# Attention backward for one decode query: two bf16 row tiles transposed as one fp32 block, and five dk stores that spare two DMA engines in place of eight

## The chip, the cores and the metric

The kernel runs on one core of a Trainium2 chip. The metric is device time in microseconds (us) of one execution; the time before is the median of three runs, 1280.13 us (1279.72 to 1282.18). The engines are named as the profile names them: PE is TensorE's matrix multiplication, PEld its weight loads, DVE is VectorE, ACT is ScalarE, POOL is GpSimd and SP is SyncE. Here SP issues the loads and POOL the stores.

## The reference

It is softmax attention with one query per head, and its backward pass. There are 2 x 32 = 64 independent heads; each has 8192 keys and values of 128 elements, all bf16.

```python
def _fwd_reference(q, k, v):          # q: 2,32,1,128   k, v: 2,32,8192,128
    scale = q.shape[-1] ** -0.5
    scores = jnp.einsum("bhqd,bhkd->bhqk", q, k) * scale
    p = _softmax(scores, axis=-1)
    return jnp.einsum("bhqk,bhkd->bhqd", p, v)

def reference(q, k, v, grad_out):
    _out, _vjp = jax.vjp(_f, q, k, v)
    return (out, *_vjp(grad_out))     # out, dq, dk, dv
```

For one head, with s = K q and dp = V g (g is the row of grad_out): p = softmax(scale s), out = p V, ds = p (dp - sum(p dp)), dq = scale ds K, dk = scale ds q^T, dv = p g^T. Each head reads K and V (2 MB each) once and writes dk and dv (2 MB each) once, so at least 537 MB move.

## The kernel before

**Tiles.** K or V of one head is one tile `kvt`, 128 partitions x 64 row tiles (NT) x 128 elements: partition p holds 64 consecutive rows of the head. There are 12 such buffers (NTILE), so loads can run six heads ahead. The gradient is written over the tile it belongs to (`outer`, L421: an outer product of the head's q or g row with the weights, on DVE, in place), and the store sends that same buffer out; a load into the buffer has to wait until that store has landed.

**Steps.** The main loop (L456) runs over steps of one chunk, 16 row tiles (CH). A head has eight steps, four chunks of K (w = 0) and four of V (w = 1). Four heads are under way at once: in one step PE does the transposes of one head, the score matmuls one step later, and the accumulations `acc` of an older head, while DVE does the outer products of an older one still. Everything in the loop is pinned to program order, so each engine works its instructions off in the order in which the loop writes them.

**One step on PE.** `transpose_chunk` (L189): 16 transposes of a 128 x 128 bf16 block each (L194). The K or V block is the stationary operand (a weight load, PEld L194), the identity the moving one. The result `tp` fills two PSUM buffers in turn; ACT copies it to SBUF as `ev` (L196). After the transposes come, where they are due, `join` (L409), then four `acc` matmuls (L372; 64 columns of the array each, so two run side by side), `spread_rows` (L228), `max_spread` (L251), and at last `score_chunk` of the step before (L208): four matmuls on 32 columns of the array each, side by side, whose moving operand is a contiguous quarter of `ev` and whose stationary operand is a 32-column window of `qdT`, in which only one column is the head's q (or g) and the rest are zeros, so that chunk c's scores fall into row c.

**The chain inside a head.** After the four K chunks `keep_raw` (L221, DVE) copies the scores out of PSUM, `spread_rows` brings them to one per partition and row tile, then come `max_part` (DVE L240), `max_all` (PE L244, an fp32 transpose of a 128 x 1 column; DVE L246), `max_spread` (PE L251, DVE L261), `expo` (ACT L271, which stands in ACT's order behind the step's copy L196; then DVE L280 fills `E_pad`), and the `acc` matmuls of the next step need `E_pad`. PE L178 (`broadcast`) writes the same PSUM tile `sw` that DVE L240 reads.

**Queues.** SP issues loads (L100) in program order, each waiting for the store that frees its buffer. POOL issues the 2 MB stores (L445). The last head's stores go out in 512 KB pieces on SP. A 128-row transfer gives each of the 16 DMA engines eight rows of 16 KB. `by_rows` (L85), used for dk of the heads in SPREAD (4, 11, ..., 53: eight of them), sends 126 rows in one transfer, nine to each of 14 engines, and two rows in a second, one to each of the two engines left out. [...]

Of the kernel before, what the change touches and what calls it, by code (L numbers as in the profile page):

```python
# [9 lines left out]
ALU = mybir.AluOpType  # L10
AX = mybir.AxisListType
BF16 = mybir.dt.bfloat16
F32 = mybir.dt.float32

CH = 16
QT = 4
CW = 64
NG = 2
SG = 4
SW = 32  # L20
NTILE = 12
FIRST = 6
SPREAD = range(4, 60, 7)


@with_exitstack
def kernel(
# [11 lines left out]
    nc = tc.nc  # L39
    B, H, Sq, D = q.shape  # L40
    Sk = k.shape[2]
    P = nc.NUM_PARTITIONS
    assert Sq == 1 and D == P
    BH = B * H
# [3 lines left out]
    NCH = NT // CH  # L48
    SL = 2 * NCH
    scale = float(D) ** -0.5  # L50
# [69 lines left out]
        load(j, 0)  # L120
        load(j, 1)

    ident_bf = const.tile([P, P], BF16)
    masks.make_identity(nc, ident_bf[:])
    ident_f = const.tile([P, P], F32)
    masks.make_identity(nc, ident_f[:])
    ones = const.tile([P, 1], F32)
    nc.vector.memset(ones[:], 1.0)
    groups = [g * P // NG for g in range(NG)]
# [8 lines left out]
    nc.vector.memset(E_pad[:], 0.0)  # L138
    nc.vector.memset(dS_pad[:], 0.0)

    sel4 = const.tile([P, NCH, SG], F32)
    nc.vector.memset(sel4[:], 0.0)
    for g in range(SG):
        nc.vector.tensor_copy(
            out=sel4[g * SW : (g + 1) * SW, :, g],
            in_=ident_f[g * SW : (g + 1) * SW, g * SW : g * SW + NCH],
        )

    Q0 = NCH - 1
    qdT = const.tile([P, 2, Q0 + NCH * BH + SW], BF16)  # L150
    nc.vector.memset(qdT[:], 0.0)
    for w in range(2):
        tps = ps_m.tile([P, BH], BF16, tag=f"acc{w}", name="tps")
        nc.tensor.transpose(tps[:], qd_nat[:BH, w, :], ident_bf[:BH, :BH])
        nc.vector.tensor_copy(
            out=qdT[:, w, Q0 : Q0 + NCH * BH].rearrange("p (i f) -> p i f", f=NCH)[:, :, 0],
            in_=tps[:],
        )

    dqT = const.tile([P, BH], BF16)  # L160
    oT = const.tile([P, BH], BF16)
# [1 line left out]
    def begin(i):  # L163
# [7 lines left out]
        h.lsum = sw[:, 2 * NT + 2 * P : 2 * NT + 2 * P + 2]  # L171
        h.mb = sw[:, 2 * NT + 2 * P + 2 : 2 * NT + 2 * P + 3]

    def broadcast(i, w):

        h = heads[i]
        pin(
            nc.tensor.matmul(  # L178
                h.qbp,
                lhsT=qdT[:, w, Q0 + NCH * i : Q0 + NCH * i + 1].to_broadcast([P, P]),  # L180
                rhs=ident_bf[:],
                start=True,
                stop=True,
            )
        )
        h.qb[w] = small.tile([P, D], BF16, tag=f"qb{w}", name="qb")
        pin(nc.vector.tensor_copy(out=h.qb[w][:], in_=h.qbp))

    def transpose_chunk(i, c):  # L189
        w, c = divmod(c, NCH)  # L190
        src = heads[i].tile[w]
        tp = ps_tp.tile([P, CH, P], BF16, tag="tp", name="tp")
        for t in range(CH):
            pin(nc.tensor.transpose(tp[:, t, :], src[:, c * CH + t, :], ident_bf[:]))  # L194
        ev = evp.tile([P, CH, P], BF16, tag="ev", name="ev")
        pin(nc.scalar.copy(out=ev[:], in_=tp[:]))  # L196
        return ev

    def score_chunk(i, c, ev):

        h = heads[i]
        w, c = divmod(c, NCH)
        if c == 0:
            h.raw = ps_sdp.tile([P, QT * P], F32, tag="raw", name="raw")
        q0 = Q0 + NCH * i - c
        for g in range(SG):
            pin(
                nc.tensor.matmul(  # L208
                    h.raw[g * SW : (g + 1) * SW, :],
                    lhsT=qdT[:, w, q0 : q0 + SW],  # L210
                    rhs=ev[:, g * QT : (g + 1) * QT, :].rearrange("p n d -> p (n d)"),
                    start=(c == 0),
                    stop=(c == NCH - 1),
                )
            )
# [7 lines left out]
    def spread_rows(i, w):  # L223

        h = heads[i]
        for t in range(QT):
            pin(
                nc.tensor.matmul(  # L228
                    h.score[w].rearrange("p (n t) -> p n t", t=QT)[:, :, t],
                    lhsT=h.rows[:, t * P : (t + 1) * P],  # L230
                    rhs=sel4[:].rearrange("p c g -> p (c g)"),
                    start=True,
                    stop=True,
                )
            )

    def max_part(i):
        h = heads[i]
        h.mp = small.tile([P, 1], F32, tag="mp", name="mp")
        pin(nc.vector.reduce_max(out=h.mp[:], in_=h.s, axis=AX.X))  # L240

    def max_all(i):
        h = heads[i]
        pin(nc.tensor.transpose(h.mT, h.mp[:], ident_f[:]))  # L244
        h.gm = small.tile([1, 1], F32, tag="gm", name="gm")
        pin(nc.vector.reduce_max(out=h.gm[:], in_=h.mT, axis=AX.X))  # L246

    def max_spread(i):
        h = heads[i]
        pin(  # L250
            nc.tensor.matmul(  # L251
                h.mb,
                lhsT=ones[0:1, :].to_broadcast([1, P]),
                rhs=h.gm[:],
                start=True,
                stop=True,
            )
        )
        h.negm = small.tile([P, 1], F32, tag="negm", name="negm")
        pin(  # L260
            nc.vector.tensor_scalar(  # L261
                out=h.negm[:], in0=h.mb, scalar1=-scale, scalar2=None, op0=ALU.mult
            )
        )

    def expo(i):
        h = heads[i]
        h.E_f = work.tile([P, NT], F32, tag="E_f", name="E_f")
        h.ld = small.tile([P, 2], F32, tag="ld", name="ld")
        pin(  # L270
            nc.scalar.activation(  # L271
                out=h.E_f[:],
                in_=h.s,
                func=ACT.Exp,
                bias=h.negm[:],
                scale=scale,
                accum_out=h.ld[:, 0:1],
            )
        )
        pin(nc.vector.tensor_copy(out=E_pad[:, 0:NT], in_=h.E_f[:]))  # L280
# [39 lines left out]
    def normalise_p(i):  # L320
        h = heads[i]
        total(h.lsum[:, 0:1], h.ld[:, 0:1])
        h.rl = small.tile([P, 1], F32, tag="rl", name="rl")
        pin(nc.vector.reciprocal(out=h.rl[:], in_=h.lsum[:, 0:1]))
        pairs(i, 1, h.E_f, h.rl[:], "p2")
        h.rls = small.tile([P, 1], F32, tag="rls", name="rls")
        pin(
            nc.vector.tensor_scalar(
                out=h.rls[:], in0=h.rl[:], scalar1=scale, scalar2=None, op0=ALU.mult
            )  # L330
        )

    def normalise_ds(i):
        h = heads[i]
        total(h.lsum[:, 1:2], h.ld[:, 1:2])
        negdelta = small.tile([P, 1], F32, tag="negdelta", name="negdelta")
        pin(
            nc.vector.tensor_scalar(
                out=negdelta[:],
                in0=h.lsum[:, 1:2],  # L340
                scalar1=h.rl[:],
                scalar2=-1.0,
                op0=ALU.mult,
                op1=ALU.mult,
            )
        )
        dSu = work.tile([P, NT], F32, tag="dSu", name="dSu")
        pin(
            nc.vector.scalar_tensor_tensor(
                out=dSu[:],  # L350
                in0=h.dp,
                scalar=negdelta[:],
                in1=h.E_f[:],
                op0=ALU.add,
                op1=ALU.mult,
            )
        )
        pin(nc.vector.tensor_copy(out=dS_pad[:, 0:NT], in_=dSu[:]))  # L358
        pairs(i, 0, dSu, h.rls[:], "ds2")

    def acc(i, w, c):

# [42 lines left out]
    def join(i, w):  # L405

        h = heads[i]
        pin(
            nc.tensor.matmul(h.acc[w][:, 0:1], lhsT=h.sel[:], rhs=ones[:], start=True, stop=True)  # L409
        )  # L410
        pin(
            nc.vector.tensor_scalar(
                out=(oT if w else dqT)[:, i : i + 1],
                in0=h.acc[w][:, 0:1],
                scalar1=(h.rl if w else h.rls)[:],
                scalar2=None,
                op0=ALU.mult,
            )
        )
# [32 lines left out]
    last = list(range(1, NCH + 1))  # L452
    AHEAD = NTILE // 2

    prev = None
    for g in range(SL * BH + O0 + NCH + 4 - SL):  # L456
        now = [(g // SL - b, g % SL + b * SL) for b in range(4)]
# [2 lines left out]
        def at(r0):  # L460

            return next((i for i, r in now if r == r0), None)
# [37 lines left out]
        if prev is not None:  # L500
            score_chunk(*prev)
        prev = (g // SL, g % SL, ev) if ev is not None else None

        if (i := at(NCH)) is not None:
            keep_raw(i)
# [16 lines left out]

    for w, (src, dst) in enumerate(((dqT, out_1), (oT, out_0))):
        tps = ps_m.tile([BH, P], BF16, tag=f"acc{w}", name="tps")
        nc.tensor.transpose(tps[:], src[:], ident_bf[:])
        nat = evp.tile([P, CH, P], BF16, tag="ev", name="nat")
        nc.vector.tensor_copy(out=nat[:BH, 0, :], in_=tps[:])
        load_eng.dma_start(out=dst.rearrange("b h s d -> (b h s) d"), in_=nat[:BH, 0, :])
# [30 lines left out]
```

## Time and profile before

| | before |
|---|---|
| median of three runs (lowest to highest) | 1280.13 us (1279.72 to 1282.18) |
| span of the profiled execution | 1280.2 us |
| mean granted TensorE clock | 0.991 |
| ACT copy ev<-tp L196 | x512, 954.5 us, 1865 ns each |
| DVE outer product L427 | x512, 616.8 us, 1216 ns each |
| PE transposes L194 | x8192, 544.4 us busy, 220 ns each (pipelined) |
| PE scores L208 | x2048, 205.2 us busy |
| PE acc L372 | x2048, 320.0 us busy |
| stores to landing (POOL, 2 MB) | 40.6 us median |
| loads to landing (SP, 2 MB) | 19.1 and 19.4 us median |
| moved | 539.03 MB, mean 421 GB/s |

The span is that of one profiled execution, and it agrees with the median of the runs to 0.1 us. Busy times are unions of records, and a PE record holds the latency of the pipeline too: 16 transposes of 220 ns each take about 0.9 us, not 3.5. How much PE really takes is therefore read from the starts of its groups in the timeline. Idle time of an engine counts only where it holds up the chain that ends last.

### The profile page before, as it was taken

The page shows a single profiled execution, that of the slowest core. Times are in us where ns is not written, and L with a number is a line of the kernel's source. Part 1 is how long each engine was busy: PE and PEld are TensorE (multiplying, and loading weights), DVE is VectorE, ACT ScalarE, POOL GpSimd, SP SyncE. Part 2 cuts the span into 40 slices and gives each one's busy share as a digit, 9 for nine tenths or more (in the row PEclk, how much of TensorE's full clock was granted, in tenths as well). Part 3 has the DMA queues.
Part 4 walks back from the last instruction along what each step waited for, and adds up shares of the span by engine and source line. Part 5 has one row for each costly group of instructions (what it writes and reads, how often), then busy time and mean ns, then how long its engine had stood idle before and what let it go on. Part 6 is the DMA issues. An engine that isn't in the chain of part 4 may idle for free.

```text
span 1280.2 us, 32473 instructions
## 1 busy us (share of the span) xinstructions
PE 1190.2 (93%) x14148; PEld 810.6 (63%) x14148; DVE 1025.8 (80%) x2256; ACT 975.3 (76%) x641; POOL 76.0 (6%) x143
## 2 busy tenths in 40 slices
PE   6999999999999999999999999999999999999994
PEld 5666666666666666666666666666666666666662
DVE  2888887888877888888888878788778888888885
ACT  6777777778777777777777777787777777777771
POOL 0000000000000000000000000000000000000000
PEclk9999999999999999999999999999999999999996
DMA  9999999999999999999999999999999999999996
GB/s 392 423 428 428 428 427 429 430 426 429 427 430 425 414 427 429 428 423 428 428 429 419 425 428 426 427 421 427 427 423 421 427 429 428 420 425 428 428 411 273
DMA packets 40155, 539.03 MB, mean 421 GB/s; under 512 B 5196, under 2 KB 5196, under 8 KB 6476
## 3 DMA queue, kind: packets, MB, share of 16 engines
q1 hardware_dynamic: 20172, 272.70, 50.1%
q0 software_dynamic: 19840, 264.25, 49.0%
q8 instruction: 110, 1.80, 0.5%
q14 instruction: 33, 0.27, 0.1%
HBM read 268.47 MB, written 268.47 MB: 419 GB/s over the span
## 4 chain that ended last, share of the span: by engine, by line
PE 59%; DVE 16%; ACT 10%; issue 10%; DMA 4%; POOL 0%; SPq 0%; ACTq 0%; POOLq 0%; DVEq 0%
PE tp L194 24%; PE acc L372 15%; ACT ev L196 9%; PE raw L208 9%; DVE kvt L427 6%; PE sw L228 4%; DVE sel L395 4%; DMA out_dram<-kvt 3%; DVE rows L221 3%; PE sw L315 3%; PE sw L178 2%; PE acc L409 2%; ACT E_f L271 1%; DVE sel L389 1%; DVE E_pad L280 1%
## 5 line engine op out<-in xcount | busy, mean ns | idle before, releaser
L196 ACT COPY ev<-tp 128x2048 bf16<-128x2048 bf16 x512 | 954.5, 1865 | 275.6 <-PE tp L194 268.9
L427 DVE TENSOR_TENSOR kvt<-qb,pair 128x2048 bf16<-128x2048 bf16 x512 | 616.8, 1216 | 0.2
L194 PE MATMUL tp<-ident_bf,kvt 128*128 128x128 bf16 x8192 | 544.4, 220 | 0.0
L194 PEld LDWEIGHTS <-kvt 128*128 128x128 bf16 x8192 | 482.4, 99 | 81.6 <-issue 80.7
L208 PE MATMUL raw<-ev,qdT 128*32 128x512 bf16 x2048 | 205.2, 391 | 1.5 <-ACT ev L196 1.5
L372 PE MATMUL acc<-kvt,E_pad 128*64 128x512 bf16 x1024 | 160.2, 393 | 24.5 <-DVE E_pad L280 24.5
L372 PE MATMUL acc<-kvt,dS_pad 128*64 128x512 bf16 x1024 | 159.8, 393 | 0.1
L228 PEld LDWEIGHTS sw<-sel,rows 128*128 128x128 f32 x1024 | 124.7, 192 | 52.4 <-DVE sel L395 25.9
L395 DVE SCALAR_TENSOR_TENSOR sel<-acc,diag,sel 128x128 f32<-128x128 f32 x384 | 134.8, 351 | 13.6
L208 PEld LDWEIGHTS <-qdT 128*32 128x32 bf16 x2048 | 53.1, 93 | 136.6 <-issue 131.8
L228 PE MATMUL sw<-sel,rows 128*128 128x16 f32 x1024 | 137.1, 266 | 0.0
L445 POOL DMA_DIRECT2D out_dram<-kvt x118 | 63.3, 536 | 1094.0 <-DVE kvt L427 555.7
L221 DVE COPY rows<-raw 128x512 f32<-128x512 f32 x128 | 88.6, 692 | 22.4 <-PE raw L208 22.4
L280 DVE CAST E_pad<-E_f 128x64 bf16<-128x64 f32 x64 | 12.5, 195 | 80.3 <-ACT E_f L271 80.3
L372 PEld LDWEIGHTS <-E_pad 128*64 128x64 bf16 x1024 | 36.1, 108 | 49.9 <-DVE E_pad L280 35.7
L178 PE MATMUL sw<-ident_bf,qdT 128*128 128x128 bf16 x128 | 28.5, 223 | 38.2 <-DVE mp L240 38.2
L246 DVE TENSOR_REDUCE gm<-sw 1x1 f32<-1x128 f32 x64 | 17.9, 279 | 55.4 <-PE sw L244 55.4
L315 PEld LDWEIGHTS sw<-ld,ones 128*128 128x128 f32 x256 | 38.1, 188 | 29.7 <-issue 15.0
L372 PEld LDWEIGHTS <-dS_pad 128*64 128x64 bf16 x1024 | 36.4, 108 | 22.3 <-DVE dS_pad L358 1.0
L315 PE MATMUL sw<-ld,ones 128*128 128x1 f32 x256 | 49.1, 261 | 0.0
L409 PE MATMUL acc<-ones,sel 128*128 128x1 f32 x256 | 43.3, 239 | 5.3 <-DVE sel L395 5.3
L389 DVE TENSOR_SCALAR sel<-acc,diag 128x128 f32<-128x128 f32 x128 | 43.8, 342 | 0.0
(49 smaller groups left out, 377.1 us busy)
## 6 DMA issues: line engine op xcount, KB each, us to landing
out_dram<-kvt POOLq DMA_DIRECT2D x118, 2048.0 KB, 40.6
kvt<-in_v_dram SPq DMA_DIRECT2D x64, 2048.0 KB, 19.1
kvt<-in_k_dram SPq DMA_DIRECT2D x63, 2048.0 KB, 19.4
out_dram<-kvt POOLq DMA_DIRECT2D x8, 2016.0 KB, 44.9
out_dram<-kvt SPq DMA_DIRECT2D x8, 512.0 KB, 10.9
kvt<-in_k_dram SPq DMA_DIRECT2D x2, 512.0 KB, 4.3
kvt<-in_k_dram SPq DMA_DIRECT2D x1, 1024.0 KB, 6.9
out_dram<-kvt POOLq DMA_DIRECT2D x8, 32.0 KB, 44.3
```

Source lines behind the costliest of these rows:

```text
L194: pin(nc.tensor.transpose(tp[:, t, :], src[:, c * CH + t, :], ident_bf[:]))
L196: pin(nc.scalar.copy(out=ev[:], in_=tp[:]))
L208: nc.tensor.matmul(h.raw[g * SW : (g + 1) * SW, :], lhsT=qdT[:, w, q0 : q0 + SW], rhs=ev[:, g * QT : (g + 1) * QT, :].rearrange("p n d -> ...
L221: pin(nc.vector.tensor_copy(out=h.rows[:], in_=h.raw[:]))
L228: nc.tensor.matmul(h.score[w].rearrange("p (n t) -> p n t", t=QT)[:, :, t], lhsT=h.rows[:, t * P : (t + 1) * P], rhs=sel4[:].rearrange("p ...
L315: nc.tensor.matmul(out, lhsT=ones[:].to_broadcast([P, P]), rhs=col, start=True, stop=True)
L372: nc.tensor.matmul(h.acc[w][g : g + CW, :], lhsT=wts[:, n0 : n0 + CW], rhs=rows[:, n0 : n0 + QT, :].rearrange("p n d -> p (n d)"), start=( ...
L389: nc.vector.tensor_scalar(out=h.sel[:], in0=block, scalar1=diag[:, 0:1], scalar2=None, op0=ALU.mult)
L395: nc.vector.scalar_tensor_tensor(out=h.sel[:], in0=block, scalar=diag[:, b : b + 1], in1=h.sel[:], op0=ALU.mult, op1=ALU.add,)
L409: nc.tensor.matmul(h.acc[w][:, 0:1], lhsT=h.sel[:], rhs=ones[:], start=True, stop=True)
L427: nc.vector.tensor_tensor(out=h.tile[w][:, n0 : n0 + CH, :].rearrange("p n (e t) -> p n e t", t=2), in0=h.qb[w][:] .rearrange("p (e t) -> ...
L445: pin(eng.dma_start(out=dst[:, b0:b1, :], in_=h.tile[w][:, b0:b1, :]))
```

## The change

There are two parts. First, two neighbouring bf16 row tiles (row n and row n + 1 of each partition, 256 elements in a row) are read as 128 fp32 elements, and one fp32 transpose moves both: 8 transposes a chunk in place of 16. Partition j of the result holds, as one fp32 word, elements 2j and 2j + 1 (mod 256) of the pair, so partitions 0 to 63 belong to row n, partitions 64 to 127 to row n + 1, and the low and the high half of the words are even and odd elements. ACT copies 128 x 1024 fp32 words instead of 128 x 2048 bf16 ones. The score matmuls read `ev` as bf16 with a step of two elements, one matmul for each of two halves of the columns and each of even and odd. The stationary operand is a new window `qwin` with two columns of `qpair` (q or g spread over the two halves of the partitions, even and odd), which ACT copies in once per head and w (`window`). `sel4`, `spread_rows` and the set-up are adapted: four more set-up transposes with their copies, and `ident_bf` is now the high half of each word of `ident_f`, so it too is read with a step of two. The seven small per-head tiles become columns of one tile `st`.

Second, SPREAD goes from `range(4, 60, 7)` (eight heads) to `range(6, 60, 12)` (heads 6, 18, 30, 42 and 54).

```diff
-SPREAD = range(4, 60, 7)
+SPREAD = range(6, 60, 12)
...
-    ident_bf = const.tile([P, P], BF16)
-    masks.make_identity(nc, ident_bf[:])
     ident_f = const.tile([P, P], F32)
     masks.make_identity(nc, ident_f[:])
+    ident_bf = ident_f[:].bitcast(BF16).rearrange("p (n e) -> p n e", e=2)[:, :, 1]
...
-    Q0 = NCH - 1
-    qdT = const.tile([P, 2, Q0 + NCH * BH + SW], BF16)
+    Q0 = 2 * NCH - 2
+    qT = const.tile([P, 2, BH], BF16)
+    qpair = const.tile([P, 2, BH, 2, 2], BF16)
+    nc.vector.memset(qpair[:], 0.0)
+    qwin = const.tile([P, 2, 2, Q0 + SW], BF16)
+    nc.vector.memset(qwin[:], 0.0)
+    qd_pair = evp.tile([P, 2, 2, 2, D // 2], BF16, tag="ev", name="qd_pair")
+    for w in range(2):
+        nc.vector.tensor_copy(out=qd_pair[:BH, w], in_=...)
+        for e in range(2):
+            tps = ps_m.tile([P, BH], BF16, tag=f"acc{e}", name="tps")
+            nc.tensor.transpose(tps[:], qd_pair[:BH, w, e]..., ident_bf[:BH, :BH])
+            for t in range(2):
+                half = slice(t * D // 2, (t + 1) * D // 2)
+                nc.vector.tensor_copy(out=qpair[half, w, :, e, t], in_=tps[half, :])
...
+    def window(i, w):
+        pin(nc.scalar.copy(out=qwin[:, w, :, Q0 : Q0 + 2], in_=qpair[:, w, i]))
...
     def transpose_chunk(i, c):
-        tp = ps_tp.tile([P, CH, P], BF16, tag="tp", name="tp")
-        for t in range(CH):
-            pin(nc.tensor.transpose(tp[:, t, :], src[:, c * CH + t, :], ident_bf[:]))
-        ev = evp.tile([P, CH, P], BF16, tag="ev", name="ev")
+        tp = ps_tp.tile([P, CH // 2, P], F32, tag="tp", name="tp")
+        for m in range(CH // 2):
+            n0 = c * CH + 2 * m
+            two = src[:, n0 : n0 + 2, :].rearrange("p n d -> p (n d)").bitcast(F32)
+            pin(nc.tensor.transpose(tp[:, m, :], two, ident_f[:]))
+        ev = evp.tile([P, CH // 2, P], F32, tag="ev", name="ev")
         pin(nc.scalar.copy(out=ev[:], in_=tp[:]))
...
     def score_chunk(i, c, ev):
-        q0 = Q0 + NCH * i - c
+        q0 = Q0 - 2 * c
+        cols = ev[:].rearrange("p m s -> p (m s)").bitcast(BF16)
+               .rearrange("p (b s e) -> p b s e", b=SG // 2, e=2)
         for g in range(SG):
+            b, e = divmod(g, 2)
             pin(
                 nc.tensor.matmul(
                     h.raw[g * SW : (g + 1) * SW, :],
-                    lhsT=qdT[:, w, q0 : q0 + SW],
-                    rhs=ev[:, g * QT : (g + 1) * QT, :].rearrange("p n d -> p (n d)"),
+                    lhsT=qwin[:, w, e, q0 : q0 + SW],
+                    rhs=cols[:, b, :, e],
...
+    window(0, 0)
+    window(0, 1)
     prev = None
     for g in range(SL * BH + O0 + NCH + 4 - SL):
...
         prev = (g // SL, g % SL, ev) if ev is not None else None
+        if (i := at(NCH + 1)) is not None and i + 1 < BH:
+            window(i + 1, 0)
+        if (i := at(1)) is not None and i > 0:
+            window(i, 1)
```

More of the change, by code (lines that the diff above doesn't have):

```diff
@@ L139 @@
     nc.vector.memset(dS_pad[:], 0.0)
-    sel4 = const.tile([P, NCH, SG], F32)
+    sel4 = const.tile([P, NCH, SG // 2, 2], F32)
     nc.vector.memset(sel4[:], 0.0)
@@ L144 @@
         nc.vector.tensor_copy(
-            out=sel4[g * SW : (g + 1) * SW, :, g],
-            in_=ident_f[g * SW : (g + 1) * SW, g * SW : g * SW + NCH],
-        )
-    Q0 = NCH - 1
-    qdT = const.tile([P, 2, Q0 + NCH * BH + SW], BF16)
-    nc.vector.memset(qdT[:], 0.0)
+            out=sel4[g * SW : (g + 1) * SW, :, g // 2, :],
+            in_=ident_f[g * SW : (g + 1) * SW, g * SW : g * SW + 2 * NCH].rearrange(
+                "p (c t) -> p c t", t=2
+            ),
+        )
+    Q0 = 2 * NCH - 2
[6 more added lines that the diff above has]
+    for w in range(2):
+        nc.vector.tensor_copy(
+            out=qd_pair[:BH, w],
+            in_=qd_nat[:BH, w, :]
+            .rearrange("p (j e) -> p e j", e=2)
+            .unsqueeze(2)
+            .to_broadcast([BH, 2, 2, D // 2]),
+        )
+        for e in range(2):
+            tps = ps_m.tile([P, BH], BF16, tag=f"acc{e}", name="tps")
+            nc.tensor.transpose(
+                tps[:],
+                qd_pair[:BH, w, e].rearrange("p t j -> p (t j)"),
+                ident_bf[:BH, :BH],
+            )
+            for t in range(2):
+                half = slice(t * D // 2, (t + 1) * D // 2)
+                nc.vector.tensor_copy(out=qpair[half, w, :, e, t], in_=tps[half, :])
     for w in range(2):
@@ L154 @@
         nc.tensor.transpose(tps[:], qd_nat[:BH, w, :], ident_bf[:BH, :BH])
[L155 to L158, printed above, removed]
+        nc.vector.tensor_copy(out=qT[:, w, :], in_=tps[:])
     dqT = const.tile([P, BH], BF16)
@@ L179, in broadcast @@
                 h.qbp,
-                lhsT=qdT[:, w, Q0 + NCH * i : Q0 + NCH * i + 1].to_broadcast([P, P]),
-                rhs=ident_bf[:],
+                lhsT=qT[:, w, i : i + 1].to_broadcast([P, P]),
+                rhs=ident_bf,
                 start=True,
@@ L204, in score_chunk @@
             h.raw = ps_sdp.tile([P, QT * P], F32, tag="raw", name="raw")
-        q0 = Q0 + NCH * i - c
+        q0 = Q0 - 2 * c
+        cols = (
+            ev[:]
+            .rearrange("p m s -> p (m s)")
+            .bitcast(BF16)
+            .rearrange("p (b s e) -> p b s e", b=SG // 2, e=2)
+        )
         for g in range(SG):
+            b, e = divmod(g, 2)
             pin(
@@ L225, in spread_rows @@
         h = heads[i]
-        for t in range(QT):
+        for m in range(QT):
             pin(
                 nc.tensor.matmul(
-                    h.score[w].rearrange("p (n t) -> p n t", t=QT)[:, :, t],
-                    lhsT=h.rows[:, t * P : (t + 1) * P],
-                    rhs=sel4[:].rearrange("p c g -> p (c g)"),
+                    h.score[w].rearrange("p (n m t) -> p n m t", m=QT, t=2)[:, :, m, :],
+                    lhsT=h.rows[:, m * P : (m + 1) * P],
+                    rhs=sel4[:].rearrange("p c b t -> p (c b t)"),
                     start=True,
@@ L238, in max_part @@
         h = heads[i]
-        h.mp = small.tile([P, 1], F32, tag="mp", name="mp")
-        pin(nc.vector.reduce_max(out=h.mp[:], in_=h.s, axis=AX.X))
+        st = small.tile([P, 8], F32, tag="st", name="st")
+        h.mp, h.gm, h.negm = st[:, 0:1], st[0:1, 1:2], st[:, 2:3]
+        h.ld, h.rl, h.rls, h.negdelta = st[:, 3:5], st[:, 5:6], st[:, 6:7], st[:, 7:8]
+        pin(nc.vector.reduce_max(out=h.mp, in_=h.s, axis=AX.X))
     def max_all(i):
         h = heads[i]
-        pin(nc.tensor.transpose(h.mT, h.mp[:], ident_f[:]))
-        h.gm = small.tile([1, 1], F32, tag="gm", name="gm")
-        pin(nc.vector.reduce_max(out=h.gm[:], in_=h.mT, axis=AX.X))
+        pin(nc.tensor.transpose(h.mT, h.mp, ident_f[:]))
+        pin(nc.vector.reduce_max(out=h.gm, in_=h.mT, axis=AX.X))
     def max_spread(i):
@@ L253, in max_spread @@
                 lhsT=ones[0:1, :].to_broadcast([1, P]),
-                rhs=h.gm[:],
+                rhs=h.gm,
                 start=True,
@@ L258, in max_spread @@
         )
-        h.negm = small.tile([P, 1], F32, tag="negm", name="negm")
         pin(
             nc.vector.tensor_scalar(
-                out=h.negm[:], in0=h.mb, scalar1=-scale, scalar2=None, op0=ALU.mult
+                out=h.negm, in0=h.mb, scalar1=-scale, scalar2=None, op0=ALU.mult
             )
@@ L268, in expo @@
         h.E_f = work.tile([P, NT], F32, tag="E_f", name="E_f")
-        h.ld = small.tile([P, 2], F32, tag="ld", name="ld")
         pin(
@@ L274, in expo @@
                 func=ACT.Exp,
-                bias=h.negm[:],
+                bias=h.negm,
                 scale=scale,
@@ L322, in normalise_p @@
         total(h.lsum[:, 0:1], h.ld[:, 0:1])
[L323 to L326, printed above, removed]
+        pin(nc.vector.reciprocal(out=h.rl, in_=h.lsum[:, 0:1]))
+        pairs(i, 1, h.E_f, h.rl, "p2")
         pin(
             nc.vector.tensor_scalar(
-                out=h.rls[:], in0=h.rl[:], scalar1=scale, scalar2=None, op0=ALU.mult
+                out=h.rls, in0=h.rl, scalar1=scale, scalar2=None, op0=ALU.mult
             )
@@ L335, in normalise_ds @@
         total(h.lsum[:, 1:2], h.ld[:, 1:2])
-        negdelta = small.tile([P, 1], F32, tag="negdelta", name="negdelta")
         pin(
             nc.vector.tensor_scalar(
-                out=negdelta[:],
+                out=h.negdelta,
                 in0=h.lsum[:, 1:2],
-                scalar1=h.rl[:],
+                scalar1=h.rl,
                 scalar2=-1.0,
@@ L351, in normalise_ds @@
                 in0=h.dp,
-                scalar=negdelta[:],
+                scalar=h.negdelta,
                 in1=h.E_f[:],
@@ L358, in normalise_ds @@
         pin(nc.vector.tensor_copy(out=dS_pad[:, 0:NT], in_=dSu[:]))
-        pairs(i, 0, dSu, h.rls[:], "ds2")
+        pairs(i, 0, dSu, h.rls, "ds2")
     def acc(i, w, c):
@@ L414, in join @@
                 in0=h.acc[w][:, 0:1],
-                scalar1=(h.rl if w else h.rls)[:],
+                scalar1=h.rl if w else h.rls,
                 scalar2=None,
@@ L524 @@
         tps = ps_m.tile([BH, P], BF16, tag=f"acc{w}", name="tps")
-        nc.tensor.transpose(tps[:], src[:], ident_bf[:])
+        nc.tensor.transpose(tps[:], src[:], ident_bf)
         nat = evp.tile([P, CH, P], BF16, tag="ev", name="nat")
```

## The prediction

> **What bounds the kernel now.** I read the page's busy times first, then who waited for whom, then PE's timeline over one head, then the table of windows at the end.
>
> ```profile
> PE 1190.2 (93%) x14148; PEld 810.6 (63%) x14148; DVE 1025.8 (80%) x2256; ACT 975.3 (76%) x641; POOL 76.0 (6%) x143
> DMA  9999999999999999999999999999999999999996
> q8 instruction: 110, 1.80, 0.5%
> ```
>
> Two candidates stand close together: PE at 93%, and DMA engines that are full in every slice but the last. In the list of waits no PE instruction waits for a load of `kvt`, so the loop runs at the pace of the engines. One head in PE's timeline:
>
> ```profile
> 641.38 1.06 PE L228 MATMUL sw<-sel,rows 128*128 128x16 f32 x8
> ...
> 643.37 0.22 PE L178 MATMUL sw<-ident_bf,qdT 128*128 128x128 bf16 x1 [0.60 <-DVE mp L240]
> ...
> 645.47 0.27 PE L244 MATMUL sw<-ident_f,mp 128*1 128x128 f32 x1
> 645.58 1.05 PE L194 MATMUL tp<-ident_bf,kvt 128*128 128x128 bf16 x16
> ...
> 649.18 0.62 PE L372 MATMUL acc<-kvt,E_pad 128*64 128x512 bf16 x4 [0.36 <-DVE E_pad L280]
> ...
> 660.82 1.06 PE L228 MATMUL sw<-sel,rows 128*128 128x16 f32 x8
> ```
>
> The period is 660.82 - 641.38 = 19.44 us. PE's groups start back to back but for two stalls a head: **stall 1**, 0.60 us, where `broadcast` waits for DVE's maximum, and **stall 2** before `acc`, whose E_pad waits for ACT. For stall 2 I take starts: transposes from 647.75 last 0.91, `acc` follows transposes elsewhere after 0.09, so it could start at 648.75 and starts at 649.18: 0.43 us. Stall 1 is a DVE chain from the end of a score group (rows, four pieces of sel, an outer product, the maximum: 639.95 to 643.33); more PE work inside it is absorbed, up to 0.60. Stall 2 is the ACT chain, seen in the chain of waits near the end (columns: start, length, what):
>
> ```profile
> 1190.21 0.91 PE tp L194 x16
> 1191.19 1.86 ACT ev L196
> 1193.06 0.32 ACT E_f L271 x2
> 1193.40 0.21 DVE E_pad L280
> 1193.65 0.62 PE acc L372 x4
> ```
>
> At the end both limits meet. Columns: window, length, PE, PEld, DVE, ACT, POOL busy, clock, DMA share, GB/s.
>
> ```profile
> 1240.00:1244.00 4.00, 4.00 (x53) 2.33 (x49) 3.65 (x6) 3.91 (x3) 0.53 (x1) 1.00 0.83 352
> 1248.00:1254.00 6.00, 4.63 (x48) 2.43 (x47) 3.80 (x9) 3.42 (x4) 0.53 (x1) 0.99 0.56 235
> 1270.00:1274.30 4.30, 0.01 (x1) 0.00 (x0) 0.35 (x2) 0.00 (x0) 0.00 (x0) 0.50 0.48 189
> ```
>
> The last line of that table shows no more compute; DMA runs at half, and from 1274.4 to 1278.0 its share is 0.06, one engine of sixteen. So compute ends at 1270.96 (the last transfer's issue), and a straggling engine ends it. That last transfer takes 8.1 us to land (page, `nat`); a 512 KB load into empty queues took 4.3. Without the straggler the run would have ended at 1280.2 - 3.8 = **1276.4**: the end that compute alone would give. The span agrees with the median of the runs, 1280.13, so no correction is made.
>
> **Part 1: the transposes.** Removed: 16 bf16 transposes a chunk, a group of 0.907 us (mean of 0.91, 0.92 and 0.89 in the chain). Added: eight fp32 ones. No row has one of full size; two rows have its halves. L244 is an fp32 transpose with 128 moving columns, in one pass (64 records for 64 heads): the next group starts 0.11 us after it (645.58 - 645.47), against 0.056 for a bf16 one (0.907 / 16). The fp32 weight load of 128 columns is in `spread_rows`:
>
> ```profile
> 20.13 0.97 PEld L228 LDWEIGHTS sw<-sel,rows 128*128 128x128 f32 x8
> ...
> 647.42 0.10 PEld L208 LDWEIGHTS <-qdT 128*32 128x32 bf16 x4
> 647.75 0.90 PEld L194 LDWEIGHTS <-kvt 128*128 128x128 bf16 x16 [0.23 <-issue]
> ```
>
> Eight loads in 0.97 with the last 0.19 long: (0.97 - 0.19) / 7 = 0.111 apart. In the bf16 stream the loads hide behind the matmuls (98 ns each, yet 16 in 0.90), and I take the same for fp32: 0.11 each. But the first load of a group does not hide: it starts at 647.75, when the score matmuls (0.33 from 647.42) are through. For bf16 that load is short; for fp32 it is 0.11 bare. New group: 0.11 + 8 x 0.11 = 0.99, **0.083 us more** than 0.907. Low end: first load hidden, 0.88, 0.03 less. High end: load and matmul never overlap, or two passes as the 1024 records of L228's 512 calls have: 0.11 + 8 x 0.22 = 1.87, 0.96 more. I take 0.083, since both halves have their own row.
>
> [...]
>
> **ACT.** The copy goes from 2048 to 1024 elements. L196 takes 1.865 us, L271 0.319 for 64 elements: 0.78 ns an element, so 1.07 us; bounds 0.32 and 1.87. It saves 0.80 on stall 2's chain: `exp` ends that much earlier, stall 2 goes to zero and PE is next. The 128 `window` copies (0.2 to 0.32 each, by L271's two rows) wait for scores that PE did one step before; behind them stands the next copy L196, with ACT idle over a quarter of the time already. Nothing; without that cover 2 x 0.32 a head.
>
> **Scores.** Same four matmuls of 512 columns, read with a step of two. No row has such a step. [...] I take no change: type and count are L208's own. The same holds for `broadcast` (at most 2 x 0.056 a head).
>
> [...]
>
> **The rest.** `spread_rows`, the tile `st` and DVE's work keep their counts, and the small tiles were written and read in one serial chain: nothing; 0.2 us a head, one small DVE operation, if a wait appears. Set-up: four more transposes and some ten small DVE copies (0.31 each at L155) between q's arrival at 8.8 and the first transposes, about +3. Against it, head 0 is ACT-bound (four copies in 7.17 us from 15.26, so 1.79 a step), and with 1.07 it becomes PE's 0.99 + 0.33: about -3 over its steps. I take 0, with -3 to +3. Tail: one copy stands in the last head's chain, -0.8.
>
> **Sum for compute.** Of eight chunks a head one lies in stall 1: 7 x 0.083 - 0.43 = +0.15 us a head; 63 heads, +9.5. 1276.4 + 9.5 - 0.8 = **1285**.
>
> **Part 2 and the DMA floor.** Removing 8192 of PE's 28296 instructions takes 8192 / 28296 of q8's 110 fetches, 32 of 16 KB. At 428 GB/s over 16 engines a 16 KB row takes 0.61 us. Three spread stores fewer: fourteen engines lose 3 rows, -1.8 us; engines 4 and 5 gain 21 rows, +12.8, and if they carry the fetches half each, lose 16, -9.8: +3.0. So DMA alone ends at 1280.2 - 1.8 = 1278.4 to 1283.2, by which engines straggle. Stores issued earlier cannot help an engine that is never idle. POOL issues six descriptors fewer, off the path (POOL 6% busy). The floor lies under 1285; compute decides.
>
> **Rivals.**
> R1, not slower: the first load of a group hides, or groups grow by less than 0.068, from where 1276.4 + 63 x (7 x 0.068 - 0.43) - 0.8 = 1278.4 is compute's end. Then the DMA floor holds: 1278.4 with the same straggler, 1278.4 - 3.6 = 1274.8 if fewer fetches even it out; 1276.5. For it: the low end above and DMA full throughout. Against it: the bare load at 647.75.
> R2, slower: the score matmuls move at half rate. [...] It decides from about 0.02 more a group. [...]
> R3: the fp32 transpose overlaps with nothing or takes two passes: 0.96 a group, of which stall 1 absorbs 0.6 once: 8 x 0.96 - 0.6 - 0.43 = 6.65 a head, x 63 = 419: 1694. Against it: L244's single pass, and loads 0.111 apart with matmuls between them.
>
> **How the numbers follow.** Forecast 0.45, R1 0.37, R2 0.10, R3 0.08. The forecast's own range: groups 0.068 to 0.10 longer with set-up's bounds, 1278 to 1292. The range 1273.5 to 1294 covers it and R1, leaving out R2 and R3, 18 in 100. A change of 0.2%, 2.6 us, is about what this measurement can tell from none. Faster: most of R1, 0.30. Same: R1's rest and the forecast's lower edge, 0.18. Slower: 0.52.
>
> **What would show it.** Group length of L194's successor, first weight load's start to the next group: 0.99 right, 0.9 R1, 1.9 R3. [...] Stall 2 gone, stall 1 smaller. [...] q8 at 78 packets. I am wrong if PE's period rises and the end does not, or the reverse.

## The result, and the profile after

The changed kernel takes **1272.03 us** (median of 4 runs, 1271.97 to 1272.97), beside 1281.16 us (1279.72 to 1283.63, 4 runs) for the kernel before: a ratio of 0.9932, 95% interval 0.9913 to 0.9952, so 9.1 us less. The forecast was 1285, and the range began at 1273.5. The profiled execution has a span of 1270.2 us, against 1280.2. Its time is 1271.98: in all the runs on record the time of an execution is 1.7 to 1.9 us longer than its span. So the execution profiled before, with a span of 1280.2, took about 1282 us, not the median of 1280.13.

The page of the changed kernel:

```profile
PE 1189.4 (94%) x10056; PEld 784.5 (62%) x10056; DVE 1030.9 (81%) x2267; ACT 557.0 (44%) x769; POOL 72.9 (6%) x138
...
q8 instruction: 79, 1.29, 0.4%
...
L222 ACT COPY ev<-tp 128x1024 f32<-128x1024 f32 x512 | 518.5, 1013 | 661.8 <-PE tp L220 656.3
```

PE has 4092 instructions fewer of each kind in the records, its instruction fetches fall from 110 to 79, and a copy takes 1.013 us in place of 1.865. PE's busy time has hardly moved (1190.2 to 1189.4), but that says nothing: it is a union of pipelined records. PE's timeline shows more (start, length, group, idle before):

```profile
645.64 1.09 PE L220 MATMUL tp<-ident_f,kvt 128*128 128x128 f32 x8
...
647.22 1.06 PE L261 MATMUL sw<-sel,rows 128*128 128x16 f32 x8
...
649.20 0.22 PE L202 MATMUL sw<-ident_f,qT 128*128 128x128 bf16 x1 [0.57 <-DVE st L275]
...
654.53 0.62 PE L401 MATMUL acc<-kvt,E_pad 128*64 128x512 bf16 x4
...
656.66 0.62 PE L401 MATMUL acc<-kvt,E_pad 128*64 128x512 bf16 x4
...
666.23 1.06 PE L261 MATMUL sw<-sel,rows 128*128 128x16 f32 x8
```

Three readings. The period of a head is 666.23 - 647.22 = 19.01 us, where it was 19.44. A full cycle of `acc`, scores and transposes is 656.66 - 654.53 = 2.13 us, where the kernel before has 2.11 (its `acc` starts at 654.34 and 656.45): in this cycle eight fp32 transposes cost PE about 0.02 us more than sixteen bf16 ones. Over all heads a group takes 0.024 us more behind scores (median from its first matmul to the next group 1.022 us, 0.998 before), 0.017 more behind the two small matmuls L347, and 0.015 to 0.020 less elsewhere; the eight groups of a head together take 0.055 us more. And the first `acc` at 654.53 no longer waits; stall 2 is gone, stall 1 stands at 0.57.

A faster period must run into something. The list of waits shows what (total us, times, longest):

```profile
PE tp L220 <- DMA kvt<-in_v_dram: 3.1, 5, 1.5
PE tp L220 <- DMA kvt<-in_k_dram: 0.6, 2, 0.4
PE acc L401 <- DVE E_pad L312: 0.6, 1, 0.6
```

The last line held 24.5 us over the 64 heads in the kernel before. The first two lines are new: PE now waits for loads, which it never did. The waits add up to only 3.7 us because the loads had a lead to lose first; in the last heads the period is 19.4 to 20.7 us, the pace of the transfers. The windows of the end (columns as before: length, PE, PEld, DVE, ACT, POOL, clock, DMA share, GB/s):

```profile
1240.00:1250.00 10.00, 3.61 (x14) 1.81 (x14) 6.84 (x13) 0.00 (x0) 0.00 (x0) 0.50 0.99 418
1250.00:1260.00 10.00, 0.00 (x0) 0.00 (x0) 0.00 (x0) 0.00 (x0) 0.00 (x0) 0.50 0.80 333
1260.00:1265.00 5.00, 0.00 (x0) 0.00 (x0) 0.00 (x0) 0.00 (x0) 0.00 (x0) 0.50 0.50 206
```

All compute is over before 1250 (in the kernel before it ended at 1270.4), and for 20 us the DMA engines alone finish what is queued, at a share of 0.80 until 1260 and of 0.50 until 1265. So **the DMA engines set the end**, and there are two questions. Why is their end at 1272, when the prediction put the DMA floor at 1278.4 to 1283.2? And which part of the change lowered it?

### The profile page after: what moved, and what is told of

Read it like the earlier page. It is cut to its first block, busy times and chain, and to the rows that moved or that the text cites. A ratio compares the mean times of both kernels' runs of the same rounds, so it can differ in the third digit from the quotient of the medians.

```text
span 1270.2 us, 24551 instructions
## 1 busy us (share of the span) xinstructions
PE 1189.4 (94%) x10056; PEld 784.5 (62%) x10056; DVE 1030.9 (81%) x2267; ACT 557.0 (44%) x769; POOL 72.9 (6%) x138
## 3 DMA queue, kind: packets, MB, share of 16 engines
q8 instruction: 79, 1.29, 0.4%
## 4 chain that ended last, share of the span: by engine, by line
PE 70%; DVE 15%; DMA 9%; another core or an unknown queue 2%; issue 2%; ACT 0%; SPq 0%; POOL 0%; DVEq 0%; ACTq 0%
PE tp L220 30%; PE acc L401 17%; PE raw L241 11%; DVE kvt L456 6%; PE sw L261 4%; DMA out_dram<-kvt 4%; DVE sel L424 4%; DMA kvt<-in_v_dram 3%; DVE rows L254 3%; PE sw L347 3%; PE sw L202 2%; DMA kvt<-in_k_dram 2%; PE sw L285 1%; DVE sel L418 1%
## 5 line engine op out<-in xcount | busy, mean ns | idle before, releaser
L222 ACT COPY ev<-tp 128x1024 f32<-128x1024 f32 x512 | 518.5, 1013 | 661.8 <-PE tp L220 656.3
L220 PE MATMUL tp<-ident_f,kvt 128*128 128x128 f32 x4096 | 548.2, 277 | 3.9 <-DMA kvt<-in_v_dram 3.1
L220 PEld LDWEIGHTS tp<-ident_f,kvt 128*128 128x128 f32 x4096 | 454.5, 144 | 84.9 <-issue 65.9
L241 PE MATMUL raw<-ev,qwin 128*32 128x512 bf16 x2048 | 209.9, 400 | 0.0
L261 PEld LDWEIGHTS sw<-sel,rows 128*128 128x128 f32 x1024 | 123.9, 191 | 52.3 <-DVE sel L424 25.9
L241 PEld LDWEIGHTS <-qwin 128*32 128x32 bf16 x2048 | 52.8, 93 | 135.3 <-issue 131.0
L280 DVE TENSOR_REDUCE st<-sw 1x1 f32<-1x128 f32 x64 | 17.9, 279 | 55.9 <-PE sw L279 55.9
L202 PE MATMUL sw<-ident_f,qT 128*128 128x128 bf16 x128 | 28.9, 226 | 36.0 <-DVE st L275 36.0
L347 PEld LDWEIGHTS sw<-st,ones 128*128 128x128 f32 x256 | 38.2, 188 | 30.8 <-issue 15.6
L347 PE MATMUL sw<-st,ones 128*128 128x1 f32 x256 | 49.1, 261 | 0.0
L438 PEld LDWEIGHTS acc<-ones,sel 128*128 128x128 f32 x256 | 39.3, 194 | 7.2 <-DVE sel L424 7.2
```

The source lines that it names most:

```text
L220: pin(nc.tensor.transpose(tp[:, m, :], two, ident_f[:]))
L241: nc.tensor.matmul(h.raw[g * SW : (g + 1) * SW, :], lhsT=qwin[:, w, e, q0 : q0 + SW], rhs=cols[:, b, :, e], start=(c == 0), stop=(c == NCH ...
L261: nc.tensor.matmul(h.score[w].rearrange("p (n m t) -> p n m t", m=QT, t=2)[:, :, m, :], lhsT=h.rows[:, m * P : (m + 1) * P], rhs=sel4[:].r ...
L347: nc.tensor.matmul(out, lhsT=ones[:].to_broadcast([P, P]), rhs=col, start=True, stop=True)
```

## The experiments

Every time below is a median beside runs of the kernel before on the same chip, which came out between 1280.84 and 1281.98 in all of them. "Eight", "five" and so on are numbers of spread stores (the dk stores that leave out two of the sixteen DMA engines; the texts on record call these two engines 4 and 5, but no trace names the engine of a packet).

**1. The two parts apart, and the compute's lead.** Each part of the change alone, and the kernel before with stall 2 taken away by other means: in the step of `expo`, ACT copies half of the chunk, then does the exponential, then copies the other half.

```diff
# e1: the changed kernel          # e2, e4: the kernel before
-SPREAD = range(6, 60, 12)        -SPREAD = range(4, 60, 7)
+SPREAD = range(4, 60, 7)         +SPREAD = range(6, 60, 12)
# e3, e4: the kernel before, transpose_chunk and the loop
+        if w == 1 and c == NCH - 1:
+            pin(nc.scalar.copy(out=ev[:, 0 : CH // 2, :], in_=tp[:, 0 : CH // 2, :]))
+            return ev, tp
...
+        if g < SL * BH and rest is not None:
+            finish_copy(ev, rest)
```

> The changed kernel with the eight spread stores of before. Theory C (the fp32 transposes take stall 2 away, compute runs ahead, and the DMA engines have stores to send until the end): 1272, at most 1274 (three more spread stores are three rows of 0.61 us on fourteen engines). Theory F (31 instruction fetches of 16 KB fewer on two engines): 1272 to 1274 too, or less, since engines 4 and 5 lose 21 more rows. Theory S (the five spread stores in place of eight are the gain): about 1281.

> The kernel before with the five spread stores of the change. Theory S: about 1272. Theory C: 1281, since compute ends where it did. Theory F: 1281 or more: engines 4 and 5 keep their fetches and get 21 rows back, up to 12.8 us, 1293.

> The kernel before, bf16 transposes and eight spread stores, but in the step of the exponential ACT copies half of the chunk, does the exponential, and copies the other half, so that E_pad is ready when PE gets to acc: stall 2 goes without any change in fetches or stores. Theory C: PE's period falls from 19.44 to about 19.0 and the time to about 1272. Theories F and S: the period falls, the time stays at 1280 to 1282.

> The same with five spread stores. Theory C: 1270 to 1274. Theory S: 1272, and below the run with eight. Theory F: 1281 or more.

| | us (lowest to highest, runs) | ratio to before, 95% |
|---|---|---|
| e1, transposes alone | 1274.85 (1272.58 to 1278.94, 9) | 0.9949, 0.9932 to 0.9967 |
| e2, five stores alone | 1276.75 (1275.36 to 1279.26, 11) | 0.9963, 0.9950 to 0.9977 |
| e3, before without stall 2 | 1281.25 (1277.93 to 1286.21, 11) | 0.9998, 0.9977 to 1.0020 |
| e4, e3 with five stores | 1276.84 (1275.40 to 1281.97, 11) | 0.9964, 0.9947 to 0.9980 |

None of the three theories holds in all four runs. Theory C falls with e3, which does to the compute what the transposes do and gains nothing. Theory S falls with e1, and theory F with e2 and e4, which gain 4.4 us each. e1, at 1274.85, lies a little above what C and F allowed. A window near the end of e3:

```profile
1260.00:1270.00 10.00, 0.00 (x0) 0.00 (x0) 0.00 (x0) 0.00 (x0) 0.00 (x0) 0.50 0.61 253
```

And from its list of waits:

```profile
PE tp L194 <- DMA kvt<-in_v_dram: 9.8, 14, 2.8
```

Its compute is done before 1260 (the last copy ends at 1257.7), about 13 us sooner than in the kernel before, PE waits for loads, and the run still takes 1281. So the transfers of the kernel before could not end earlier than 1281 with eight spread stores, whatever the compute did: a faster compute is not why e1 is faster. In e4 PE waits for loads too (9.6 us on V, 4.0 on K, in a trace of its slowest execution, 1281.97), in e2 not at all. Since e4, with the faster compute, is no faster than e2, the two limits of the kernel before seem to meet near 1276.8 with five stores.

**2. How the number of spread stores sets the time.**

> The changed kernel with no spread store at all. Theory P (the two engines left out carry the instruction fetches, half each, as the prediction's sum has it): engines 4 and 5 get 35 rows of 0.61 us back, 21 us, and with their 79 fetches they end far behind: 1283 to 1293. Theory N (the fetches do not sit on two engines, and a spread store only costs the other fourteen): 1272 less five times 0.6 to 1.5: 1264 to 1269.

> The kernel before with no spread store. Theory P: 110 fetches and 56 rows back on two engines, 34 us: 1295 to 1310. Theory N: 1281 less eight times 0.6 to 1.5: 1269 to 1276.

> The changed kernel with three spread stores (heads 10, 30, 50). Theory P, if engines 4 and 5 are not yet the last ones with five: below 1272 by two times 0.6 to 1.5, 1269 to 1271, else up to 1282 (14 rows of 0.61 us back). Theory N: 1267 to 1271.

> The changed kernel with four spread stores (heads 8, 23, 38, 53) instead of five. Theory of two limbs: the time is the later of engines 4 and 5, which fell by 3.55 us a spread store in the changed kernel (1284.75 with none, 1274.1 with three), and of the other fourteen, which rose by 0.94 (1272.03 with five, 1274.85 with eight). By the first limb four give 1284.75 - 4 x 3.55 = 1270.6, by the second 1272.03 - 0.94 = 1271.1: so 1271, 0.5 to 1.5 us less than with five. Rival, no limbs: the number between three and eight does nothing but scatter, 1272 to 1274.

| spread stores | 0 | 3 | 4 | 5 | 8 |
|---|---|---|---|---|---|
| kernel before | 1294.30 (e6) | | | 1276.75 (e2) | 1281 |
| changed kernel | 1284.75 (e5) | 1274.10 (e7) | 1271.57 (e9) | 1272.03 | 1274.85 (e1) |

The intervals of the ratios: e5 1.0018 to 1.0038, e6 1.0086 to 1.0120, e7 0.9931 to 0.9956, e9 0.9901 to 0.9929 (five of its six runs lie between 1270.04 and 1271.92, one at 1282.22). Theory N falls: with no spread store both kernels are slower, e5 within theory P's range and e6 0.7 us under it; e7 is in P's wider range only. The time falls by 3.55 us a spread store in the changed kernel up to about four (10.65 / 3; in the kernel before by at least 17.55 / 5 = 3.5, because its run with five is already held by something else), and rises beyond: the changed kernel by 2.82 / 3 = 0.94 us a store from five to eight, the kernel before by 4.4 / 3 = 1.5.

This is the curve of **two limbs**: the engines that are left out shed work, the other fourteen take it on, and the time follows the later. Counting rows at 0.61 us, as the prediction did, gives the fourteen 0.61 us a store; the end moves by half as much again, or more than double.

The packets of the traces fit this. During the later spread stores some packets are slow: of the 2048 8 KB packets of the stores, 51 take more than 0.4 us in place of 0.309 in the kernel before (13 of 1280 in the changed kernel), and 16 KB ones take up to 2.15 in place of 0.611. What rows took beyond those times during the spread stores (60 ns or more each, all engines together) is 75 us in the kernel before, 24 in e2, 35 in e1 and 20 in the changed kernel. From five stores to eight, and shared by fourteen engines, that is an estimated (75 - 24) / 3 / 14 = 1.2 us a store before and (35 - 20) / 3 / 14 = 0.36 after, on top of the row's own 0.61. These are single executions, but the order is that of 1.5 and 0.94. Four stores were forecast at 1271, and the run agrees, but it is not told apart from five.

What makes these packets slow no run shows. Rows in nines alone do not make them so: the first two spread stores of the kernel before, e1, e2 and the changed kernel send rows in the same nines and have at most two packets of 256 over 0.4 us, where the third has 6 to 19.

**3. Do instruction fetches cost the rest?** The first try added 7936 small memsets to POOL's program in the changed kernel (16 behind each outer product), the second 7888 empty instructions to SP's in e1's (68 behind each load): about as many bytes to fetch as the transposes saved (the queue q14 of the profile moved 0.79 and 0.78 MB in place of 0.28, where q8 had fallen from 1.80 to 1.29).

```diff
# e8, outer                                    # e10, load; e11 and e12 with 17 in place of 68
+            for _ in range(16):               +        if i >= NTILE // 2:
+                pin(store_eng.memset(         +            for _ in range(68):
+                    idle[:], 0.0))            +                pin(load_eng.drain())
```

> The changed kernel with 7936 more instructions in GpSimd's program, which write zeros to one unused column 16 at a time between the stores (about 0.1 us each, GpSimd is 6% busy): 0.5 MB more instruction fetches, as much as the change took away, with PE, ACT, DVE and the stores as they are. Theory F (fewer fetches are what the fp32 transposes bring): up by 3 to 7, 1275 to 1279. Theory M (it is something else in the fp32 transposes, ACT's or PE's traffic): 1272 to 1273.

e8 took 1415.61 us (ratio 1.1033 to 1.1063) and tells nothing of fetches. POOL's timeline shows why:

```profile
600.11 9.99 POOL L469 MEMSET idle<- 128x1 f32 x64
610.54 0.53 POOL L478 DMA_DIRECT2D out_dram<-kvt  x1 [0.43 <-issue]
```

64 memsets take 9.99 us, 0.156 each, so POOL issues a store every 10.96 us, and two a head make 21.9: POOL had become the bound. The experiment was mis-sized.

> The changed kernel with eight spread stores (1274.85 before this), and 7888 empty instructions on SyncE, 68 behind each of 116 loads: some 0.5 MB more to fetch, as much as the transposes saved, with no traffic of TensorE, ScalarE or VectorE. Theory F (fetching instructions costs all DMA engines, so the fetches saved are what the fp32 transposes bring with eight spread stores too): 1280 to 1281.5, as the kernel before. Theory G (fetches sit on engines 4 and 5 alone, which with eight spread stores have about 18 us of room, 1284.75 - 8 x 3.55 = 1256; the gain comes from something else the transposes changed): 1274 to 1275.8. In both the share of the instruction queues rises by some 0.2 points of sixteen engines' time. If an empty instruction takes SyncE more than 0.14 us (9.9 us a load by 68), loads are late and the run tells nothing.

e10 took 1304.51 us (1296.41 to 1308.98, 6 runs; ratio 1.0139 to 1.0200), 29.7 us more than e1 and far beyond both theories. Near its end:

```profile
1290.00:1300.00 10.00, 0.00 (x0) 0.00 (x0) 0.00 (x0) 0.00 (x0) 0.00 (x0) 0.50 0.09 38
```

A share of 0.09 is about one engine and a half of sixteen, and from 1293 to the end the packets show a single one at work. So the empty instructions of SP hold up one DMA engine above all. It is not alone: over all engines, rows took 25.9 us an engine beyond their 0.611, where they took 9.1 in e1, most of it during the spread stores. Which engine is it? A quarter of them, with five and with eight spread stores:

> The changed kernel (five spread stores, 1272.0) with 1972 empty instructions on SyncE, 17 behind each of 116 loads. Theory X: what empty instructions of SyncE cost lies on one DMA engine, and that one is of the two that a spread store leaves out. 7888 of them cost 29.7 us with eight spread stores, where that engine had 1274.85 - (1284.75 - 8 x 3.55) = 18.5 us of room, so 48.2 us in all, and a quarter costs 12.0. With five it stands at 1284.75 - 5 x 3.55 = 1267.0, so 1279.0 now, 7 us over the 1272.0 before: 1277 to 1281. Theory Y: the engine is one of the other fourteen or the cost lies on all, so there is no room: a quarter of 29.7, 7.4 us, gives 1279.4 here as well; the next run tells the two apart.

> The changed kernel with eight spread stores (1274.85) and the same 1972 empty instructions. Theory X: the engine stands at 1256.3 and now at 1268.3, under 1274.85, so nothing is seen: 1273.8 to 1276.0, and less than with five spread stores. Theory Y: no room, 7.4 us more: 1282.3, 1280.5 to 1284.

With five: 1276.46 (1275.41 to 1279.26, 9 runs; ratio 0.9941 to 0.9975), 4.4 us more than without them. With eight: 1273.89 (1273.37 to 1275.27, 6 runs; ratio 0.9914 to 0.9951), no more than e1's 1274.85. The same instructions cost something with five spread stores and nothing with eight; eight is now better than five. So **the loaded engine is one of the two that a spread store leaves out**: theory X holds and Y falls. The size was a little under the forecast (1276.46, not 1277 to 1281).

The packets show that engine in every run. The traces do not name a packet's engine, but each packet starts some 4 ns before the one ahead of it on its engine ends, so the chains can be followed. On one engine, called the marked one here, nearly every 16 KB row takes 5 to 60 ns longer than 0.611 us; in a spread store that engine gets about two 8 KB packets, where the others get eighteen. Rows of this kind between 100 and 1100 us, added up from the packet records of the traces:

```
kernel                  instructions   rows   extra us   extra ns a row
before                        32473    1413       32.3      22.9
e2 before, five               32470    1482       33.2      22.4
after                         24551    1446       26.4      18.3
e5 after, none                24546    1462       25.3      17.3
e10 after, 7888 more          32442    1474       33.4      22.6
```

The extra follows the number of instructions of the program, of PE (before against after) and of SP (e10) alike: about 1.3 ns each (between 100 and 1100 us the three kernels execute 26,002, 20,073 and 25,961). The marked engine also carries most of SP's fetches: in e10 the instruction queue beside PE's, q14, has 96 packets where the kernel before has 33, and 68 of the 91 that could be followed stood beside such slow rows, without the empty instructions 10 of 32. PE's fetches do not sit there: in the kernel before only 4 of 104 that could be followed stood beside such a row. What lengthens these rows no run shows; every run here was recorded, so none tells whether the recording has a part in it.

**4. TensorE's side or ScalarE's?** Left open is why the transposes gain 6.4 us with eight spread stores, where the marked engine has room. ACT's old copy was put back (the same bits as 2048 bf16 elements), with eight and with five:

```diff
-        pin(nc.scalar.copy(out=ev[:], in_=tp[:]))
+        pin(nc.scalar.copy(out=ev[:].bitcast(BF16), in_=tp[:].bitcast(BF16)))
```

> The changed kernel with eight spread stores (1274.85), the copy of a transposed chunk done again as 2048 bf16 elements (the same bits) in place of 1024 fp32: ScalarE as in the kernel before, 1.87 us a copy, stall 2 back and the period of the compute near 19.4 us; TensorE's instructions and their number as changed. Theory F (the gain lies with TensorE's instructions and their fetches): 1274 to 1276, under which the period of the compute, 19.4, still lies (19.85 from the loads). Theory G (it lies with ScalarE's copies or the lead they give): 1280 to 1282, as the kernel before.

> The same copy in the changed kernel with five spread stores (1272.0). Theory F: 1271.5 to 1273.5, up to 1 us for the last head's copy, which is 0.85 us longer. Theory G: 1276 to 1278, as the kernel before with five spread stores (1276.75).

e13: 1275.98 (1275.81 to 1280.52, 12 runs; ratio 0.9939 to 0.9975). Theory F holds: the gain with eight stores is TensorE's, but for 1.1 us. e14: 1276.48 (1275.84 to 1276.66, 9 runs; ratio 0.9951 to 0.9977), which looks like theory G, 4.4 us more than with the short copy. Its own profile decides. On its page the long copy:

```profile
L222 ACT COPY ev<-tp 128x2048 bf16<-128x2048 bf16 x512 | 954.7, 1866 | 253.2 <-PE tp L220 239.3
```

A window near its end:

```profile
1240.00:1250.00 10.00, 9.43 (x82) 5.90 (x82) 8.69 (x16) 7.90 (x5) 0.53 (x1) 1.00 0.75 321
```

And a line of its waits:

```profile
PE acc L401 <- DVE E_pad L312: 22.5, 64, 1.4
```

Stall 2 is back, PE never waits for a load, and from 1240 to 1250 the DMA engines are a quarter idle while PE is at 9.43 of 10: here the **compute** sets the end, at 1276. It does so in e2, whose row for the same window is

```profile
1240.00:1250.00 10.00, 9.33 (x115) 6.34 (x111) 8.14 (x16) 7.91 (x5) 0.53 (x1) 1.00 0.78 331
```

In e13 the times say the same, nine of twelve between 1275.81 and 1276.62; its trace is of the slowest execution (1280.52), in which the compute ended at 1271.2 and transfers at 1278.9. So no effect of the copy's traffic is needed: ScalarE's shorter copy counts because it takes the compute's limit out of the way.

**What lowered the transfers' end with eight stores.** Mean time of a DMA engine in us, added up from all packets of each trace (neighbouring records overlap by 4 ns, some 9 us in every sum; only differences count):

```
                                      before   after   e1 (eight)   e2 (before, five)
rows at 0.611 us for 16 KB            1252.3  1252.1       1252.3              1252.1
what rows took beyond that              12.5     7.8          9.1                 9.5
PE's instruction fetches                 6.6     4.7          4.7                 6.6
other fetches and small packets          3.9     3.7          3.9                 3.8
sum                                   1275.3  1268.5       1270.0              1272.0
end of the last packet                1280.4  1270.4       1274.7              1274.3
```

From before to e1 the sum falls by 5.3 us and the end by 5.7. 1.9 of it are 31 fetches fewer at 0.96 us each, shared by sixteen engines (a fetch of PE is a 16 KB packet that takes 0.96 us). 3.4 are rows that took less. By estimate 31 x 0.40 / 16 = 0.8 of it are rows directly behind a fetch (such a row takes about 1.0 us), and 0.3 the marked engine. Most of the rest lies in the spread stores, (75 - 35) / 16 = 2.5 with their share of the fetches, and that part scatters: e3, with the transposes and stores of the kernel before, has 53 us there in place of 75, and 10.7 in the second row in place of 12.5. From before to the changed kernel the sum falls by 6.8, and 3.2 us more come from a more even end. So by this estimate about 3.0 of the 5.3 us go with the number of PE's instructions; why rows in the spread stores take less with fp32 transposes, if they do, stays open. No run added fetches of PE alone, and none tells the number of its instructions from their fp32 form.

## Why the prediction was wrong, point by point

- **"The end that compute alone would give", 1276.4:** near the mark, by luck. Three runs that the compute bounds took 1276.75 (e2), 1276.48 (e14) and 1275.98 (e13). But 1276.4 was worked out from a span, and its time would be some 1.8 us more; in spans e2 and e14 end at 1274.3 and 1274.1. The other error ran the opposite way: with free queues the last transfer lands after 1.8 us (e14), not 4.3, and 1280.2 - (8.1 - 1.8) = 1273.9. The forecast 1285 and the DMA floor are sums from the same span, so as times both would stand 1.8 us higher than written, and the miss is that much larger. And the straggler was not something apart from the bound: e3 ended its compute about 13 us sooner and still took 1281. The transfers were the bound.
- **The transposes, "For bf16 that load is short; for fp32 it is 0.11 bare":** the first step that failed. Behind scores the group grew by 0.024 us, not 0.083, and 0.007 on the mean of a head's eight: the matmuls follow each other at the 0.11 us taken from L244, but in the trace's records the second weight load of a group starts 57 ns after the first, about half of L228's 0.111. L228 multiplies in two passes (1024 records for its 512 calls), and its spacing was no measure of a load alone. Both lie under the 0.068 from where R1 was to hold.
- **ACT, stall 2, scores, windows:** right. The copy takes 1.013 (1.07 was expected), stall 2 went to zero, the score group stands at 0.34 us between its first weight load and that of the transposes (0.33 before), and nobody waits for a window. Reading `ev` with a step of two elements costs a score group those 0.01 us. R2 and R3 fall; no row of the kernel before had such a step, and the 0.10 on R2 was the author's estimate.
- **The compute sum, +9.5 us:** with the measured 0.055 for a head's groups in place of 7 x 0.083 the working's own sum is 0.055 - 0.43 = -0.38 us a head, and 19.01 - 19.44 = -0.43 was measured (stall 1 also shrank by 0.03). Its sign was wrong: the sum had compute end the run at 1285, and compute is over before 1250.
- **The DMA floor, "1278.4 to 1283.2":** the second step that failed, and the one that sets the measured time, as R1 said it would. Two terms were mis-sized. Three spread stores fewer were to take 1.8 us off fourteen engines; they take 2.8 with fp32 transposes, and 4.4 in the kernel before. (The 7 rows that a store takes off each of the two engines were priced at 7 x 0.61 = 4.3 us; it was 3.55.) And for the fourteen engines the transposes were put at nothing, their fetches priced as 0.61 us rows on the two engines left out alone, half each (which two of the sixteen those are, the "engines 4 and 5" of the sum, and that they carry PE's fetches, no run shows); PE's 31 fetches fewer (32 predicted) are packets of 0.96 us that do not sit on the marked engine (in the kernel before 4 of 104 stood beside its slow rows), and the transfers end 6.4 us sooner for the transposes (e1). 2.8 and 6.4 make the 9.1 us measured. What of the 6.4 is not fetches stays open.
- **R1** had the mechanism, the DMA floor, and PE did wait for `kvt` (3.7 us) at a period under 19.4 (19.01); its 1276.5 and its low end of 1274.8 came from the same mis-sized floor. The overall range missed by 1.5 us.

The account in one line: transfers bound the kernel before at 1281; the transposes alone, partly by fewer instruction fetches, bring them to 1274.85, five stores bring that to 1272.03, and the short copy keeps the compute, at 1276 without it, from taking over.

## What to carry to other kernels

Where an engine and the DMA engines are both as full as here (PE at 93%, the DMA engines at 90% or more in every slice but the last), a floor of the transfers needs a measurement of its own: take the compute's wait away (e3) and see whether the end moves, before a sum over the compute decides the forecast. Price a transfer that is spread unevenly by a run without it (e5, e6), not by counting rows. Keep spans and times apart in one sum. And count instructions: here PE's fetches took 6.6 us of a DMA engine's time on the mean before and 4.7 after, and 1972 empty instructions on SP moved the end by 4.4 us (e11) or by nothing (e12), according to the room on the engine that they load.

## What was not expected of the hardware

- One DMA engine's rows grow with the number of instructions that the program executes, by about 1.3 ns an instruction (in 1000 us 32.3 us for 26,002 instructions before, 26.4 for 20,073 after, 33.4 for 25,961 in e10). 7888 empty instructions on SP moved the end by 29.7 us.
- A PE instruction fetch of 16 KB holds its DMA engine for 0.96 us and the row behind it for about 1.0, where a row of the same size takes 0.611.
- A store of 126 rows over fourteen engines moved the end by 0.94 us (changed kernel) to 1.5 us (before) from five stores to eight, not by the 0.61 of one row more, and the first two such stores of a run show hardly any of the slow packets (at most two of 256 over 0.4 us).
- A group of eight fp32 transposes of 128 x 128 costs PE from 0.02 us less to 0.024 us more than sixteen bf16 ones, for the same bytes.
